# A third scratch tile for the swapped product, a fourth stage-matrix tile, and one reordered step in a long-convolution kernel

## The chip, the cores and the metric

The kernel runs on one core of a Trainium2 chip, in one launch. The metric is the device time of that launch in microseconds. Three runs of the kernel before took 1143.68, 1144.38 and 1144.84 us; the median, 1144.38 us, is the time before. The engines are called as in the profile: PE multiplies matrices (PEld is its weight loading), DVE, ACT and POOL work elementwise, and SP issues the DMAs.

## What is computed

For each of 8 batches, a causal convolution of 6400 positions by 128 channels with a filter of the same length, written in the reference with Fourier transforms, then a 5-tap convolution along the sequence whose sigmoid gates a projection, and an output projection:

```python
Yf = np.fft.rfft(x, n=2 * S, axis=1) * np.fft.rfft(h, n=2 * S, axis=0)[None]
y = np.fft.irfft(Yf, n=2 * S, axis=1)[:, :S, :]
for k in range(K):
    gate_pre += conv_w[k][None, None, :] * yp[:, k:k + S, :]
out = (1 / (1 + np.exp(-gate_pre)) * (y @ w_val)) @ w_out
```

Here `yp` is `y` with four rows of zeros ahead. Everything is float32.

## The kernel before, in words

The 6400 positions are laid out as 100 by 64, and the transform and its inverse are done as matrix products of size 100 and 64.

**Forward, first stage** (`Forward.group`, 16 groups for each batch): PE multiplies a group of input channels with the table `r1`; ACT and DVE copy the result into the big tile `gy`. **Forward, second stage and product** (`Product`, 13 blocks of 8 frequencies for each batch, the last one of 4): PE multiplies `gy` with the stage matrix of the block, a 512 KB tile that a DMA brings into one of the `m2_sb` tiles (`m2_load`). The result lies in a pair of PSUM banks (`ps2`, two pairs). Then it is multiplied with the filter's spectrum as complex numbers: `swap` (ACT, two instructions) writes the result with halves exchanged into a scratch tile `w_t`; `mul_u` (DVE) multiplies the PSUM pair with the first half of the spectrum into `gy`; `mul_t` (DVE) multiplies the scratch in place with the second half; `add` (POOL, on DVE for the last block) adds the scratch to `gy`. The two halves of the spectrum come by DMA from DRAM into two of the four `h_sb` tiles (`h_load`). `mul_u` waits for `swap`, since both read the same PSUM pair, and the block after the next needs that pair, so it waits for `mul_u`.

**Inverse, first stage** (`s3_quad`, 32 for each batch): PE multiplies `gy` with `r3`, and ACT and DVE copy the result into the tile `dt`. These are run in one loop with the forward groups of the next batch. **Inverse, last stage, and gates** (`Chunk`, 13 chunks of rows: the head (rows 60 to 63) first, then 12 chunks of 5 rows): `s4` is the last stage of the inverse, 8 or 10 pairs of PE instructions into one of four single PSUM banks (`ps1`). `copies` (ACT) writes the first tap into the gate's cells, the result `y` itself, and for all but the head a fourth tap into a tile `p_t`. `taps` (DVE, three instructions, more at borders) adds taps to the cells, and ends with an addition of `p_t` on POOL. `project` (PE) multiplies `y` with w_val, `sigm` (ACT) takes the sigmoid of the cells, `gate` (DVE) multiplies the two, `output` (PE) multiplies with w_out, and `store` copies the result out of PSUM with ACT and sends it out by DMA.

Where `y` and the gate's cells lie depends on `LATE`. Rows below it use places in `dt` that the chunk has already read; rows from it on use the tiles `yl_*` and `gl`, since the next batch's inverse begins to fill `dt` while their chunks are still at work.

The loop over chunks (steps `s` = 0 to 12) writes the order of every engine by hand; each engine runs its instructions in that order. In step `s` stand the product's PE part of block `s + 1` with a load of the stage matrix `M2B` blocks further on, `project` of chunk `s - 2`, `s4` of chunk `s`, `output` of chunk `s - 3`, `store` of `s - 4`, `swap` of block `s + 1`, `sigm` of `s - 2`, `copies` of `s`, `mul_u` of block `s`, `taps` of `s - 1`, `mul_t` and `add` of block `s`, the spectrum's load for block `s + 2`, and `gate` of `s - 2`. Step 0 has blocks 0 and 1. The products belong to the next batch, so the last of the eight batches has none. What is left of the last chunks (`finish`) is run between the first groups of the next batch.

The head of the program does the filter's own transform (`Spectrum`, 13 blocks) and the first batch's products in one loop of 13 steps, with four PSUM pairs; `hd` in DRAM keeps the spectrum.

Of the kernel before, what the change touches and what calls it, by code (L numbers as in the profile page):

```python
# [9 lines left out]
F32 = mybir.dt.float32  # L10
# [5 lines left out]
C = 128  # L16
N1 = 100
# [3 lines left out]
KB = 8  # L21
# [6 lines left out]
CH = 5  # L28
HEAD = (60, 4)
CHUNKS = [HEAD] + [(a, CH) for a in range(0, 60, CH)]  # L30
NCH = len(CHUNKS)
OUT_ORDER = CHUNKS[1:] + [HEAD]
LATE = 30
LATER = 7
M2B = 3
HB = 4
XB = 4

# [62 lines left out]
def longconv_moe(ctx: ExitStack, tc: tile.TileContext, x, h, r1, m2, r3, m4, w64, out):  # L101
# [4 lines left out]
    cp = ctx.enter_context(tc.tile_pool(name="cp", bufs=1))  # L106
# [12 lines left out]
    w_sb = cp.tile([C, NW], F32, name="w_sb")  # L119
    wc_sb = w_sb[:, 2 * C :]  # L120
    gl = cp.tile([128, N2 - LATE, N1], F32, name="gl")
    yl = {a: cp.tile([128, CH, N1], F32, name=f"yl_{a}") for a, _ in CHUNKS if a >= LATE}
    m2_sb = [cp.tile([128, KB, C], F32, name=f"m2_{i}") for i in range(M2B)]
    h_sb = [cp.tile([128, KB * C], F32, name=f"h_{i}") for i in range(HB)]
    x_sb = [cp.tile([PX, XG, N2], F32, name=f"x_{i}") for i in range(XB)]
    w_t = [cp.tile([128, KB * C], F32, name=f"w_{i}") for i in range(2)]
    p_t = [cp.tile([128, CH, N1], F32, name=f"p_{i}") for i in range(2)]
    hd = dp.tile([NKB, 2, 2 * N2, KB * C], F32, name="hd")

# [70 lines left out]
    class Forward:  # L200


        def __init__(self, src, dst):
            self.src, self.dst, self.n, self.i = src, dst, 0, 0
# [31 lines left out]
    def count(kb):  # L236
        return min(KB, N1 - kb * KB)

    def m2_load(kb):
        if kb < NKB:  # L240
            n = count(kb)
            nc.sync.dma_start(m2_sb[kb % M2B][:, :n], m2[:, kb * KB : kb * KB + n])

    def h_load(kb):
        if kb < NKB:
            n = count(kb) * C
            for r in range(2):
                nc.sync.dma_start(h_sb[(2 * kb + r) % HB][:, :n], hd[kb, r, :, :n])

    def h_double(kb):  # L250
        n = count(kb) * C
        for r in range(2):
            nc.sync.dma_start(hd[kb, r, N2:, :n], hd[kb, r, :N2, :n])

    def kdt(t, kb):
        n = count(kb)
        return t[:, : n * C].rearrange("p (d k t) -> p d k t", k=n, t=2)

    def s2_mm(src, kb):
        pt = pair()  # L260
        n = count(kb)
        for k in range(n):
            nc.tensor.matmul(
                pt[:, k // 4, (k % 4) * C : (k % 4 + 1) * C],
                lhsT=m2_sb[kb % M2B][:, k, :],
                rhs=src[:, :, kb * KB + k],
                start=True,
                stop=True,
            )
        if n <= 4:  # L270
            return pt[:, 0, : n * C].rearrange("p (k d t) -> p d k t", t=2, d=C // 2)
        return pt.rearrange("p b (k d t) -> p d (b k) t", t=2, d=C // 2)
# [24 lines left out]
    class Product:  # L297
        def __init__(self, kb, h=None):
            self.kb, self.v = kb, s2_mm(gy, kb)
            self.t = kdt(w_t[kb % 2], kb)  # L300
            self.u = gy[:, :, kb * KB : kb * KB + count(kb)]
            self.h = [kdt(i, kb) for i in h or [h_sb[(2 * kb + r) % HB] for r in range(2)]]

# [14 lines left out]
    def s3_quad(d0):  # L318
        pt = single()
        for q in range(4):  # L320
            d = d0 + q
            nc.tensor.matmul(
                pt[:N1, q * 2 * N2 : (q + 1) * 2 * N2],
                lhsT=gy[:, d // 2, :, d % 2],
                rhs=r3_sb,
                start=True,
                stop=True,
            )
        o = dv[:N1, :, :, d0 : d0 + 4].rearrange("p n c d -> p (n c) d")
        return lambda e: e(o, pt[:N1].rearrange("p (d m) -> p m d", d=4))  # L330
# [6 lines left out]
    def cells(x, n):  # L337

        out, i = [], 0
        while i < n:  # L340
            y = x + i
            end = 4 if y < 4 else LATE if y < LATE else N2
            k = min(n - i, end - y)
            s = (y - 4) % N2
            out.append((i, gl[:, y - LATE : y - LATE + k] if y >= LATE else dv[:, s : s + k, 1, :N1]))
            i += k
        return out

    class Chunk:


        def __init__(self, b, ch):
            self.b, self.ch = b, ch
            a, n = ch
            self.y = yl[a][:, :n] if a >= LATE else dv[:, a : a + n, 0, :N1]

# [91 lines left out]
    for f in (fh, fx):  # L448
# [8 lines left out]
        if f is fh:  # L457
            next(wgen)
    for kb in range(M2B):
        m2_load(kb)  # L460
    nc.sync.dma_start(r3_sb, r3)
    sp, pr = {0: Spectrum(0)}, {}
    for kb in range(-1, NKB + 1):
        if 0 <= kb < NKB:
            pr[kb] = Product(kb, sp[kb].h)
            m2_load(kb + M2B)
        if kb + 2 < NKB:
# [40 lines left out]
    def m4_load(a, k):  # L508
        k = N2 + 1 if k == N2 else k
        nc.sync.dma_start(m4_sb[:, a:k], m4.rearrange("k (n t) -> k n t", t=N1)[:, a:k])  # L510
# [5 lines left out]
    for b in range(B):  # L516
        nxt = b + 1 < B


        if trail:  # L520
            trail.pop(0)()
        if nxt:
            for kb in range(M2B):
                m2_load(kb)
            for kb in range(2):
                h_load(kb)
        for g in range(NG):
            e = [s3_quad(8 * g), s3_quad(8 * g + 4)]
            f = fx.group() if nxt else []
            e[0](act)  # L530
            e[1](dve)
            for i in f:
                i(act if g % 2 else dve)
            if trail:
                trail.pop(0)()
            if b == 0:
                m4_load(4 * g, 4 * g + 4)
                if LATER + g < NKB:
                    h_double(LATER + g)
                next(wgen, None)  # L540
                next(wgen, None)
        for _ in wgen:
            pass
        if b + 2 < B:
            fx = Forward(x[b + 2], gy)


        gs = Gates(b)
        ps = {}
        for s in range(NCH):  # L550
            if s == 0:
                gs.cs[0].s4()
                if nxt:
                    ps[0] = Product(0)
                    m2_load(M2B)
                    ps[0].swap()
            if nxt and s + 1 < NKB:
                ps[s + 1] = Product(s + 1)
                m2_load(s + 1 + M2B)
            gs.each("project", s - 2)  # L560
            if s:
                gs.cs[s].s4()
            gs.each("output", s - 3)
            gs.each("store", s - 4)
            if s + 1 in ps:
                ps[s + 1].swap()
            gs.each("sigm", s - 2)
            gs.cs[s].copies()
            if nxt:
                ps[s].mul_u()  # L570
            if s:
                gs.cs[s - 1].taps()
            if nxt:
                ps[s].mul_t()
                ps.pop(s).add()
                h_load(s + 2)
            gs.each("gate", s - 2)
            if s == 10 and b + 2 < B:
                fx.load(XB)
        trail = [lambda s=s, gs=gs: gs.finish(s) for s in range(NCH, NCH + 5)]  # L580
# [46 lines left out]
```

## Time and profile before

| | |
|---|---|
| median of three runs | 1144.38 us |
| the profiled execution | 1145.32 us, of which 1143.5 us are the profile's span |
| PE busy | 1063.3 us (93%) |
| DVE busy | 835.2 us (73%) |
| ACT busy | 725.4 us (63%) |
| POOL busy | 410.9 us (36%) |
| mean granted clock of PE | 0.988 |

All instructions of the kernel are issued through one helper, so they all carry line 88 (89 in the changed kernel), and groups are told apart by engine, operation and tiles: `pt<-gy,m` is a product's PE part, `pt<-m_sb,dt` is `s4`, `pt<-dt,w_sb` with 500 elements is `project` or `output`, `w<-pt` is `swap`, `gy<-pt,h` is `mul_u`, `w<-w,h` is `mul_t`, `gy<-gy,w` is `add`. In the timeline a row has its start, its length, the engine, the operation with its tiles and shapes, the number of instructions merged in the row (a PE product counts twice), and in brackets how long the engine stood idle before it and what released it. A PE row's length reaches into the next row by a little, since matmuls are pipelined; the time from one row's start to the next is what a piece costs.

### The profile page before, as it was taken

The page shows a single profiled execution, that of the slowest core. Times are in us where ns is not written, and L with a number is a line of the kernel's source. Part 1 is how long each engine was busy: PE and PEld are TensorE (multiplying, and loading weights), DVE is VectorE, ACT ScalarE, POOL GpSimd, SP SyncE. Part 2 cuts the span into 40 slices and gives each one's busy share as a digit, 9 for nine tenths or more (in the row PEclk, how much of TensorE's full clock was granted, in tenths as well). Part 3 has the DMA queues.
Part 4 walks back from the last instruction along what each step waited for, and adds up shares of the span by engine and source line. Part 5 has one row for each costly group of instructions (what it writes and reads, how often), then busy time and mean ns, then how long its engine had stood idle before and what let it go on. Part 6 is the DMA issues. An engine that isn't in the chain of part 4 may idle for free.

```text
span 1143.5 us, 19606 instructions
## 1 busy us (share of the span) xinstructions
PE 1063.3 (93%) x7480; PEld 946.2 (83%) x7480; DVE 835.2 (73%) x1176; ACT 725.4 (63%) x1188; POOL 410.9 (36%) x220
## 2 busy tenths in 40 slices
PE   8987899999999899999999999999999999999998
PEld 8977898769988699777987699886997789876975
DVE  5799776975589755896569855887568956698375
ACT  5787347764478546774568655775567744786365
POOL 0044004750067301770047500773018700475022
PEclk9999899989999999999999999999999999999999
DMA  5696947974199634986279741997349862793012
GB/s 148 193 326 196 333 129 257 286 210 150 44 310 279 238 90 137 297 240 213 57 243 297 221 150 55 307 265 237 89 142 296 235 214 56 251 290 111 26 28 89
DMA packets 105163, 221.15 MB, mean 193 GB/s; under 512 B 40170, under 2 KB 49358, under 8 KB 104910
## 3 DMA queue, kind: packets, MB, share of 16 engines
q1 hardware_dynamic: 105070, 219.89, 60.6%
q8 instruction: 60, 0.98, 0.4%
q14 instruction: 33, 0.27, 0.1%
HBM read 183.42 MB, written 39.32 MB: 195 GB/s over the span
## 4 chain that ended last, share of the span: by engine, by line
PE 54%; ACT 18%; POOL 12%; DVE 9%; issue 4%; DMA 3%; POOLq 0%; DVEq 0%; SPq 0%; ACTq 0%
PE pt L88 54%; POOL gy L88 7%; ACT w L88 7%; DVE dt L88 4%; POOL dt L88 3%; ACT dt L88 3%; DVE gl L88 3%; DMA m<-m 2%; ACT yl L88 2%; ACT p L88 2%; ACT gl L88 2%; DVE gy L88 1%; ACT gy L88 1%; DVE w L88 1%; POOL gl L88 1%
## 5 line engine op out<-in xcount | busy, mean ns | idle before, releaser
L88 PEld LDWEIGHTS pt<-m_sb,dt 100*128 100x128 f32 x2048 | 242.7, 193 | 71.9 <-ACT dt L88 29.6
L88 POOL TENSOR_TENSOR gy<-gy,w 128x1024 f32<-128x1024 f32 x96 | 228.0, 2375 | 148.7 <-DVE w L88 141.1
L88 PE MATMUL pt<-m_sb,dt 100*128 100x100 f32 x2048 | 247.9, 277 | 24.9 <-ACT dt L88 14.5
L88 PEld LDWEIGHTS pt<-r_sb,gy 128*100 128x100 f32 x2048 | 240.3, 172 | 30.9 <-issue 20.6
L88 PE MATMUL pt<-r_sb,gy 128*100 128x128 f32 x2048 | 248.0, 274 | 15.2 <-DVE gy L88 8.9
L88 ACT COPY dt<-pt 100x512 f32<-100x512 f32 (+3 forms) x264 | 153.8, 582 | 160.5 <-PE pt L88 159.2
L88 PEld LDWEIGHTS pt<-gy,m 128*128 128x128 f32 x1600 | 196.7, 190 | 33.1 <-DVE gy L88 12.2
L88 PE MATMUL pt<-r_sb,x 100*128 100x200 f32 x1152 | 217.1, 336 | 4.5 <-DMA x<-hl 4.2
L88 PE MATMUL pt<-gy,m 128*128 128x128 f32 x1600 | 204.7, 280 | 10.8 <-DVE gy L88 10.8
L88 DVE COPY dt<-pt 100x512 f32<-100x512 f32 (+2 forms) x168 | 116.7, 695 | 123.4 <-PE pt L88 120.9
L88 PEld LDWEIGHTS pt<-r_sb,x 100*128 100x128 f32 x1152 | 194.0, 193 | 4.7 <-issue 4.7
L88 ACT COPY gy<-pt 64x400 f32<-64x400 f32 x256 | 124.4, 486 | 100.7 <-PE pt L88 98.5
L88 DVE COPY gy<-pt 64x400 f32<-64x400 f32 x256 | 146.5, 572 | 42.8 <-PE pt L88 40.3
L88 ACT ACTIVATE w<-pt 64x1024 f32<-64x1024 f32 (+1 forms) x104 | 102.7, 988 | 103.7 <-POOL gy L88 84.1
L88 POOL MEMSET dt<- 128x4 f32 x8 | 0.8, 106 | 419.8 <-PE pt L88 419.8
L88 DVE TENSOR_TENSOR gy<-pt,h 128x1024 f32<-128x1024 f32 (+1 forms) x100 | 117.5, 1174 | 46.2 <-ACT w L88 45.9
L88 DVE SCALAR_TENSOR_TENSOR gl<-pt,w_sb,gl 128x500 f32<-128x500 f32 (+3 forms) x192 | 126.3, 661 | 15.8 <-POOL gl L88 4.9
L88 POOL TENSOR_TENSOR gl<-gl,p 128x500 f32<-128x500 f32 (+1 forms) x56 | 99.2, 1772 | 84.0 <-DVE gl L88 81.6
L88 DVE SCALAR_TENSOR_TENSOR dt<-pt,w_sb,dt 128x500 f32<-128x500 f32 (+3 forms) x192 | 115.1, 617 | 12.6 <-POOL dt L88 5.2
L88 DVE TENSOR_TENSOR w<-w,h 128x1024 f32<-128x1024 f32 (+1 forms) x100 | 122.3, 1223 | 0.0
L88 POOL TENSOR_TENSOR dt<-dt,p 128x500 f32<-128x500 f32 (+3 forms) x56 | 85.7, 1531 | 73.3 <-DVE dt L88 61.5
L88 ACT COPY w<-pt 64x1024 f32<-64x1024 f32 (+1 forms) x104 | 101.0, 971 | 2.4
(31 smaller groups left out, 741.6 us busy)
## 6 DMA issues: line engine op xcount, KB each, us to landing
h<-hd SPq DMA_DIRECT2D x168, 512.0 KB, 5.7
m<-m SPq DMA_DIRECT2D x96, 512.0 KB, 5.4
x<-xl SPq DMA_DIRECT2D x128, 224.0 KB, 2.8
out<-dt SPq DMA_DIRECT2D x48, 250.0 KB, 5.2
out<-yl SPq DMA_DIRECT2D x48, 250.0 KB, 3.0
hd<-h SPq DMA_DIRECT2D x10, 512.0 KB, 4.9
x<-hl SPq DMA_DIRECT2D x16, 224.0 KB, 2.6
h<-hd SPq DMA_DIRECT2D x14, 256.0 KB, 4.5
```

The source lines that it names most:

```text
L88: return self._tc.keep_in_program_order(call(*args, **kwargs))
```

## The change

Three things change. `M2B` is 4 and `w_t` has three tiles instead of two (`WB`), so `swap` of a block uses the scratch of the block three before. To make room, `LATE` is 35 instead of 30: `gl` has 29 rows instead of 34, the tile `yl_30` is gone, and the chunk at row 30 keeps `y` and its cells in `dt`; the head's `yl` tile has 4 rows instead of 5. And in step 1 `s4` of chunk 1 stands ahead of the product's PE part of block 2.

```diff
-LATE = 30
+LATE = 35
 LATER = 7
-M2B = 3
+M2B = 4
+WB = 3
...
-    yl = {a: cp.tile([128, CH, N1], F32, name=f"yl_{a}") for a, _ in CHUNKS if a >= LATE}
+    yl = {a: cp.tile([128, n, N1], F32, name=f"yl_{a}") for a, n in CHUNKS if a >= LATE}
...
-    w_t = [cp.tile([128, KB * C], F32, name=f"w_{i}") for i in range(2)]
+    w_t = [cp.tile([128, KB * C], F32, name=f"w_{i}") for i in range(WB)]
...
-            self.t = kdt(w_t[kb % 2], kb)
+            self.t = kdt(w_t[kb % WB], kb)
...
+            if s == 1:
+                gs.cs[s].s4()
             if nxt and s + 1 < NKB:
                 ps[s + 1] = Product(s + 1)
                 m2_load(s + 1 + M2B)
             gs.each("project", s - 2)
-            if s:
+            if s > 1:
                 gs.cs[s].s4()
```

On PE, at the start of the second batch's chunk loop (steps 0 to 2; `pt1` is a single PSUM bank, `pt2` a pair, `m4_sb` the table of `s4`), there stands before:

```order
L88 MATMUL pt1_2134<-m4_sb_68,dt_67 128x100 x8
L88 MATMUL pt2_2143<-gy_66,m2_0_80 128x128 x8
L88 MATMUL pt2_2155<-gy_66,m2_1_81 128x128 x8
L88 MATMUL pt2_2176<-gy_66,m2_2_82 128x128 x8
L88 MATMUL pt1_2186<-m4_sb_68,dt_67 128x100 x10
L88 MATMUL pt2_2213<-gy_66,m2_0_80 128x128 x8
```

On PE, at the same place of the changed kernel, there stands:

```order
L89 MATMUL pt1_2136<-m4_sb_68,dt_67 128x100 x8
L89 MATMUL pt2_2145<-gy_66,m2_0_79 128x128 x8
L89 MATMUL pt2_2157<-gy_66,m2_1_80 128x128 x8
L89 MATMUL pt1_2178<-m4_sb_68,dt_67 128x100 x10
L89 MATMUL pt2_2189<-gy_66,m2_2_81 128x128 x8
L89 MATMUL pt2_2215<-gy_66,m2_3_82 128x128 x8
```

The ten pairs of the second chunk's last stage have moved ahead of the third block, and the fourth block reads a fourth stage-matrix tile, not the first one again.

On ACT, in steps 1 and 2 of the same loop (`w` is the scratch, `p` the fourth tap), there stands before:

```order
L88 ACTIVATE w_0_91<-pt2_2176 64x1024
L88 COPY w_0_91<-pt2_2176 64x1024
L88 ACTIVATE dt_67<-pt1_2186,w_sb_71 128x5x100
L88 COPY dt_67<-pt1_2186 128x5x100
L88 ACTIVATE p_0_93<-pt1_2186,w_sb_71 128x500
L88 ACTIVATE w_1_92<-pt2_2213 64x1024
```

On ACT, at the same place of the changed kernel, there stands:

```order
L89 ACTIVATE w_2_93<-pt2_2189 64x1024
L89 COPY w_2_93<-pt2_2189 64x1024
L89 ACTIVATE dt_67<-pt1_2178,w_sb_71 128x5x100
L89 COPY dt_67<-pt1_2178 128x5x100
L89 ACTIVATE p_0_94<-pt1_2178,w_sb_71 128x500
L89 ACTIVATE w_0_91<-pt2_2215 64x1024
```

The order on ACT is the same; the third block's `swap` writes a scratch of its own, and the fourth block's writes the first block's.

On SP, at the end of each batch's chunk loop (`xl` is the batch after the next, `out` the result), there stands before:

```order
L88 DMA x_3_90<-xl 112x512
L88 DMA out<-yl_30_74 128x500
L88 DMA out<-yl_35_75 128x500
L88 DMA out<-yl_40_76 128x500
L88 DMA m2_0_80<-m2 128x1024
```

On SP, at the same place of the changed kernel, there stands:

```order
L89 DMA x_3_90<-xl 112x512
L89 DMA out<-dt_67 640x1x100
L89 DMA out<-yl_35_74 128x500
L89 DMA out<-yl_40_75 128x500
L89 DMA m2_0_79<-m2 128x1024
```

The chunk at row 30 leaves from `dt`, in pieces of 100 numbers, at the place in the queue that its own tile had.

## The prediction

> **What bounds the kernel now.** I read the page first, then busy time by stretch, then PE in order of time through one batch's chunk loop, then the chain of waits there. Of the page's busy times:
>
> ```profile
> PE 1063.3 (93%) x7480; PEld 946.2 (83%) x7480; DVE 835.2 (73%) x1176; ACT 725.4 (63%) x1188; POOL 410.9 (36%) x220
> ```
>
> PE leads over the whole span, so at most some 80 us (1143.5 less 1063.3) can be won by filling its idle time. Where is it? Four stretches: the head's product loop, the opening of the second batch's chunk loop (from its first `s4` to block 8's product), the middle of that loop, and the opening in the first batch.
>
> ```profile
> core 0: us, PE busy (x) PEld busy (x) DVE busy (x) ACT busy (x) POOL busy (x), PEclk, DMA share, GB/s
> 55.50:119.50 64.00, 45.90 (x365) 44.15 (x363) 62.91 (x53) 48.72 (x50) 28.49 (x12) 0.92 0.81 262
> 307.93:349.18 41.25, 37.32 (x281) 33.07 (x281) 31.30 (x43) 31.54 (x47) 23.87 (x13) 1.00 0.80 264
> 349.18:372.22 23.04, 23.04 (x161) 19.37 (x160) 21.06 (x27) 19.18 (x29) 18.38 (x10) 1.00 0.93 276
> 171.35:213.92 42.57, 37.65 (x281) 33.13 (x281) 31.30 (x43) 32.87 (x48) 23.84 (x13) 1.00 0.78 260
> ```
>
> In the head DVE is busy for 62.91 of 64.00 us: DVE is the bound there. In the middle of the chunk loop PE is busy without a gap, four steps in 23.04 us, 5.76 each, while DVE needs 5.27, ACT 4.80 and POOL 4.60 (each sum by four). Only in the opening does no engine fill the stretch. These are PE's rows of it, with four rows of the full pace behind, and the loop's end:
>
> ```profile
> 307.93 2.00 PE L88 MATMUL pt<-m_sb,dt 100*128 100x100 f32 x16
> 309.87 3.96 PE L88 MATMUL pt<-gy,m 128*128 128x128 f32 x32
> 315.38 2.12 PE L88 MATMUL pt<-gy,m 128*128 128x128 f32 x16 [1.54 <-DVE gy L88]
> 317.33 2.37 PE L88 MATMUL pt<-m_sb,dt 100*128 100x100 f32 x20
> 319.54 2.04 PE L88 MATMUL pt<-gy,m 128*128 128x128 f32 x16
> ...
> 336.72 1.08 PE L88 MATMUL pt<-dt,w_sb 128*128 128x500 f32 x2 [0.21 <-DVE dt L88]
> 339.29 2.48 PE L88 MATMUL pt<-m_sb,dt 100*128 100x100 f32 x20 [1.49 <-ACT dt L88]
> ...
> 346.00 2.48 PE L88 MATMUL pt<-m_sb,dt 100*128 100x100 f32 x20 [0.68 <-ACT dt L88]
> ...
> 349.18 2.02 PE L88 MATMUL pt<-gy,m 128*128 128x128 f32 x16
> 351.03 1.00 PE L88 MATMUL pt<-dt,w_sb 128*128 128x500 f32 x2
> 351.87 2.37 PE L88 MATMUL pt<-m_sb,dt 100*128 100x100 f32 x20
> 354.08 1.03 PE L88 MATMUL pt<-dt,w_sb 128*128 128x500 f32 x2
> 354.94 2.00 PE L88 MATMUL pt<-gy,m 128*128 128x128 f32 x16
> ...
> 377.12 1.00 PE L88 MATMUL pt<-yl,w_sb 128*128 128x500 f32 x2
> 379.17 2.48 PE L88 MATMUL pt<-m_sb,dt 100*128 100x100 f32 x20 [1.05 <-ACT yl L88]
> ```
>
> PE stands idle four times in the opening. The third block's product waits 1.54 us for `mul_u` of block 0. The others wait for DVE and ACT, which are late. Why are they late? The chain of waits says it, and the list of who waited for whom sums it:
>
> ```profile
> 325.47 1.97 POOL dt L88
> 327.43 2.35 POOL gy L88
> 329.81 1.03 ACT w L88
> ```
>
> ```profile
> ACT w L88 <- POOL gy L88: 84.1, 74, 2.8
> PE pt L88 <- DMA m<-m: 8.9, 7, 2.8
> ```
>
> `add` on POOL (2.35) releases `swap` on ACT, because `swap` of block k+2 writes the scratch that `add` of block k reads. Behind that `swap` on ACT stand `sigm` and `copies`, which `gate` and `taps` on DVE wait for. ACT spends 84.1 us so.
>
> **The change part by part.** *The third scratch.* `swap` of block k+3 now waits for `add` of block k, a whole step sooner. The 84.1 us go from ACT. What is late next on ACT: `sigm` of a chunk waits for POOL's last tap, the row at 325.47, which ends before the `add` that `swap` waited for. So `sigm` can start 2.35 us sooner, with the `swap` (two instructions of about 1 us) already behind it. After that nothing but PE sets the pace, since each other engine needs under 5.3 us in a step of 5.76.
>
> *The moved `s4`.* The two blocks from 309.87 cost two times 1.88, to 313.7. `s4` of chunk 1 (317.33 to 319.54, 2.21) fills 313.7 to 315.9; the third block could start at 315.38, so it comes about 0.6 later than before, and the pair of them ends at 317.9 instead of 319.54. Behind the third block stand its `swap` (ACT) and, on SP, its stage-matrix load and the spectrum loads behind it: all 0.6 us later. The spectrum loads issued between 312 and 349 us land so long after their issue:
>
> ```profile
> DMA to landing us min/median/max: 4.2/5.9/7.8
> ```
>
> The load behind the moved one was issued at about 318 and is wanted by `mul_u` of block 3 at about 325.6; 318.5 and 7.8 is 326.3 at the worst, 0.7 late on DVE. PE wants that `mul_u`'s end only at 327.2, so it costs PE up to 0.3. DVE's own rows give the next limit:
>
> ```profile
> 319.65 1.21 DVE L88 TENSOR_TENSOR w<-w,h 128x1024 f32<-128x1024 f32 x1
> 321.12 1.23 DVE L88 TENSOR_TENSOR gy<-pt,h 128x1024 f32<-128x1024 f32 x1 [0.25 <-ACT w L88]
> ```
>
> `mul_u` of block 2 starts when `mul_t` is done, 320.87, and ends at 322.1; PE comes to the fifth block at 322.0. A wait of 0.1.
>
> *The opening's sum.* At the full pace a product costs 1.85 (349.18 to 351.03), `project` 0.84, `s4` 2.21, `output` 0.86. From the first `s4` to block 8 stand 8 products (14.8), 6 `s4` (13.3), the head's `s4` of 1.94 (307.93 to 309.87), 4 `project` (3.4) and 3 `output` (2.6): 36.0. With the waits just named, 0.1 and 0.3, and another 0.4 for the restarts I take 36.8. The gain is 41.25 less 36.8, 4.45 us, in each of the batches 1 to 6. Its bounds are 3.9 (PE's busy time of 37.32 kept, which counts pipelined ends) and 5.2 (the bare 36.0). The first batch's opening takes 42.57, so 5.8. Sum: 6 × 4.45 + 5.8 = 32.5.
>
> *The clock.* Batch 4 (the first is batch 0) lost more at the place that is 339.29 in batch 1:
>
> ```profile
> 737.35 4.38 PE L88 MATMUL pt<-m_sb,dt 100*128 100x100 f32 x20 [1.49 <-ACT dt L88]
> ```
>
> ```profile
> 732.00:744.50 12.50, 10.80 (x51) 8.65 (x50) 11.18 (x15) 9.74 (x15) 9.29 (x5) 0.73 0.87 272
> ```
>
> The same ten pairs take 4.38 instead of 2.48, and the granted clock of that stretch is 0.73. I take it that PE's idle time just ahead lowered it. With the idle time gone the 1.9 us go too. The Trainium skill ("TensorE: Matmul & The Clock Gate", Part 1) says that the clock falls after an idle window of about 3.4 us; here it fell after gaps of 1.49 and 0.21 us, so by that rule the slow stretch isn't owed to them and the 1.9 us would stay: 1114.4 in place of 1112.5.
>
> *The loop's end.* In the changed build `project` of chunk 10 (377.12 here) waits for the `store` that `s4` of chunk 12 (379.17) waited for, so the idle time comes one piece earlier, 0.84 us, with ACT about 0.5 us sooner. I charge 0.35 us in each of 7 batches: −2.4. Bounds: −0.84 and +1.05 for each.
>
> *The fourth stage-matrix tile.* PE waited for these loads 8.9 us, all in the head. DVE hides it there (62.91 of 64.00). I cost it at nothing; without that cover it would be a gain of up to 8.9. In the chunk loop no wait for `m` stands in the list. At the start of each batch one more load of 512 KB goes ahead of the `x` loads on SP, which are issued four groups early.
>
> *`LATE` at 35.* The same instructions, other places. The chunk at row 30 leaves from `dt`, so the first copy of the next batch's inverse into `dt` now waits for that transfer:
>
> ```profile
> 374.06 9.83 SPq L88 DMA_DIRECT2D out<-yl  x3
> 386.44 0.58 ACT L88 COPY dt<-pt 100x512 f32<-100x512 f32 x1 [2.39 <-PE pt L88]
> ```
>
> ```profile
> out<-dt SPq DMA_DIRECT2D x48, 250.0 KB, 5.2
> ```
>
> Issued at 374.06 and 5.2 long it lands at 379.3, 7.1 us ahead. Nothing; without the cover 1 us in each of 7 batches for each microsecond late.
>
> *Sum.* 32.5 + 1.9 − 2.4 = 32.0. The profiled execution took 1145.3 us (1143.5 of span), so it would take 1113.3. It lies 0.9 above the median of the runs, so the forecast is **1112.5 us**. About 0.2%, 2.3 us, is what a measurement of this kernel can tell from no change.
>
> **The rivals.** *Transfers become the bound of the opening* (chance 0.2). The DMA share is 0.80 over 41.25 us, 33 us of work, nearly all of it behind block 0's product at 312; an opening of 36.8 leaves 32.7 us for it. For: the share is 0.93 even at the full pace. Against: a spectrum tile is asked for two steps before it is wanted, less the 1.2 us of `mul_u`: 7.1 us at the shortest steps (4.16, from 315.38 to 319.54), 10.3 at the full pace, and 7.8 is the longest landing. If landings grow by 2 us, some 1.7 us of each opening come back: 12 us, 1124.
>
> *The wait only moves to `sigm`* (0.05): POOL's tap is as late as its `add` was, and only the 1.54 us of the moved `s4` are won, 7 times, 10.8: 1133.5. Against: the tap's row ends 2.35 us before the `add`'s.
>
> *DVE and POOL collide* (0.03), the case that ends slower. One row each at the head's end:
>
> ```profile
> 115.84 2.37 POOL L88 TENSOR_TENSOR gy<-gy,w 128x1024 f32<-128x1024 f32 x1 [1.47 <-DVE w L88]
> 116.24 2.52 DVE L88 TENSOR_TENSOR w<-w,h 128x512 f32<-128x512 f32 x1
> ```
>
> A `mul_t` of half size, so at most 1.21, took 2.52 while POOL's `add` ran: 1.3 or more lost. If every `mul_t` met an `add` so, DVE's step would be 6.6 against PE's 5.76, 0.8 × 12 steps × 7 batches = 67 us, on top of 1112.5: 1179.5. It decides from 0.4 us a step (32.0 + 2.3, over 84 steps), where DVE's step passes 6.2. Against: `mul_t` of two blocks lie a DVE step of 5.3 apart and `add` follows the first at once with 2.37, so POOL must fall 2.5 us behind. The Trainium skill ("SBUF — State Buffer", Who interferes with whom) has it that a DVE instruction with two SBUF inputs and a POOL instruction that reads SBUF lock each other out for a whole instruction; the two rows agree.
>
> *The change does nothing* (0.02): the opening is bound by PE after all, 1144. The idle times in brackets speak against it.
>
> **How the numbers follow.** My forecast has the remaining 0.70; 1112.5 is its value. Its own bounds: openings at 5.2 (+4.5), the first batch's likewise 0.8, the loop's end at nothing (+2.4): 1105 with them; 3.9 instead of 4.45 and the clock not regained: 1118. To hold 8 in 10 I reach down to 1104 and up into the transfers' case, 1126. Faster by over 0.2%: 0.95 (0.70 + 0.2 + 0.05); within: 0.02; slower: 0.03.
>
> **What would show it.** Right: in the changed trace no wait of ACT `w` for POOL `gy` in the chunk loop; PE from the first `s4` to block 8 in about 36.8 us; the head unchanged at 64 us though the wait for `m` is gone; no slow clock in an opening. Wrong: DVE waits for `h` transfers in the openings, a `mul_t` much over 1.22, or the first ACT `dt` copy of a batch waiting for `out`.

## The result and the profile after

| | before | after |
|---|---|---|
| median, us | 1144.03 (1142.93 to 1144.84) | 1119.32 (1117.42 to 1120.04) |
| the profiled execution, its span | 1145.32, 1143.5 | 1117.42, 1115.5 |
| mean granted clock | 0.988 | 0.992 |

The ratio is 0.9776, with a 95% interval of 0.9763 to 0.979: 24.7 us less by the medians, 27.9 by the profiled executions; 1112.5 had been forecast, with a range from 1104 to 1126. The comparison of the profiles goes by the 27.9. The other three runs of the changed kernel took 1.4 to 2.6 us more than its profiled one; they have no trace, so where these lie stays open.

The page's busy times, and three stretches with the columns of the prediction's table: the head, the second batch's opening, and the first batch's opening.

```profile
PE 1053.5 (94%) x7480; PEld 942.9 (85%) x7480; DVE 831.8 (75%) x1176; ACT 729.7 (65%) x1188; POOL 410.7 (37%) x220
```

```profile
54.00:119.00 65.00, 45.82 (x372) 43.65 (x371) 62.90 (x53) 49.26 (x51) 28.47 (x12) 0.93 0.79 252
301.80:338.46 36.66, 36.60 (x281) 33.16 (x281) 30.16 (x42) 32.07 (x47) 23.14 (x13) 1.00 0.84 281
171.29:209.28 37.99, 36.73 (x280) 33.17 (x281) 31.45 (x44) 33.39 (x48) 24.42 (x13) 1.00 0.82 279
```

PE's share of the span is 94%, 93% before. The opening is 36.66 us long, and PE is busy for 36.60 of them. The head is still DVE's, 62.90 us of work. PE's rows of the opening, up to block 8's product, carry no idle time in brackets:

```profile
301.80 2.00 PE L89 MATMUL pt<-m_sb,dt 100*128 100x100 f32 x16
303.74 3.96 PE L89 MATMUL pt<-gy,m 128*128 128x128 f32 x32
307.54 2.37 PE L89 MATMUL pt<-m_sb,dt 100*128 100x100 f32 x20
309.75 3.90 PE L89 MATMUL pt<-gy,m 128*128 128x128 f32 x32
...
338.46 2.00 PE L89 MATMUL pt<-gy,m 128*128 128x128 f32 x16
```

The moved `s4` stands at 307.54, and the third block starts 7.95 us after the first row, where it started 7.45 after it. In the list of waits ACT's wait for POOL's `add` is gone, and ACT's `swap` waits for PE instead. PE's waits for ACT's `dt` copies fell from 19.6 to 9.4 us, but those for ACT's `yl` copies rose from 15.7 to 19.1:

```profile
ACT w L89 <- PE pt L89: 40.4, 57, 2.2
PE pt L89 <- ACT yl L89: 19.1, 20, 1.4
PE pt L89 <- ACT dt L89: 9.4, 15, 1.2
```

Nearly all of these waits of PE lie at the loop's end, from block 12 on:

```profile
361.50 1.08 PE L89 MATMUL pt<-gy,m 128*128 128x128 f32 x8
363.07 1.11 PE L89 MATMUL pt<-yl,w_sb 128*128 128x500 f32 x2 [0.49 <-ACT dt L89]
364.02 2.37 PE L89 MATMUL pt<-m_sb,dt 100*128 100x100 f32 x20
...
368.67 1.10 PE L89 MATMUL pt<-yl,w_sb 128*128 128x500 f32 x2 [1.41 <-ACT yl L89]
...
373.92 1.11 PE L89 MATMUL pt<-yl,w_sb 128*128 128x500 f32 x2 [1.08 <-ACT yl L89]
...
377.42 1.12 PE L89 MATMUL pt<-r_sb,gy 128*100 128x128 f32 x8 [0.68 <-ACT dt L89]
```

Three `project`s wait there (chunks 9, 10 and 11), where before `s4` of chunk 12 and the `project` of chunk 11 waited, 1.05 and 1.08 us; the quad's wait was there before, too. From block 12 to the next batch's first `s4` the changed kernel takes 69.47 us in every full batch, the kernel before 68.41: each end lost 1.06.

Added up by stretches of the two profiles: six openings 27.7 us (4.57 each, 4.84 in the last of them), the first opening 4.6, the slow clock in batch 4 1.8, seven loop ends −7.4, a slow clock in batch 0's end that is gone 2.6, a slow clock in the last batch that is new −1.3: 28.0, the difference of the spans.

### The profile page after: what moved, and what is told of

Same layout as the page of the kernel before. It is cut to its first block, busy times and chain, and to the rows that moved or that the text cites. A ratio compares the mean times of both kernels' runs of the same rounds, so it can differ in the third digit from the quotient of the medians.

```text
span 1115.5 us, 19581 instructions
## 1 busy us (share of the span) xinstructions
PE 1053.5 (94%) x7480; PEld 942.9 (85%) x7480; DVE 831.8 (75%) x1176; ACT 729.7 (65%) x1188; POOL 410.7 (37%) x220
## 4 chain that ended last, share of the span: by engine, by line
PE 82%; ACT 9%; DVE 5%; issue 2%; DMA 1%; POOL 0%; POOLq 0%; ACTq 0%; SPq 0%; DVEq 0%
PE pt L89 82%; ACT yl L89 2%; ACT w L89 2%; ACT dt L89 2%; DVE w L89 1%; ACT p L89 1%; DVE gy L89 1%; ACT gl L89 1%; ACT gy L89 1%; DVE h L89 1%; DVE dt L89 1%; DVE gl L89 0%; DMA x<-xl 0%; DMA x<-hl 0%; POOL dt L89 0%
## 5 line engine op out<-in xcount | busy, mean ns | idle before, releaser
L89 ACT COPY dt<-pt 100x512 f32<-100x512 f32 (+3 forms) x280 | 163.1, 583 | 164.4 <-PE pt L89 163.1
L89 PE MATMUL pt<-m_sb,dt 100*128 100x100 f32 x2048 | 243.7, 274 | 3.5 <-DVE dt L89 2.6
L89 PE MATMUL pt<-gy,m 128*128 128x128 f32 x1600 | 201.7, 279 | 2.1 <-DVE dt L89 1.6
L89 DVE SCALAR_TENSOR_TENSOR dt<-pt,w_sb,dt 128x500 f32<-128x500 f32 (+7 forms) x216 | 132.6, 630 | 11.4 <-POOL dt L89 5.3
L89 DVE SCALAR_TENSOR_TENSOR gl<-pt,w_sb,gl 128x500 f32<-128x500 f32 (+2 forms) x168 | 108.8, 651 | 22.1 <-issue 9.9
L89 POOL TENSOR_TENSOR dt<-dt,p 128x500 f32<-128x500 f32 (+1 forms) x64 | 101.4, 1585 | 52.5 <-DVE dt L89 40.5
L89 PE MATMUL pt<-dt,w_sb 128*128 128x500 f32 (+2 forms) x240 | 115.3, 571 | 1.2 <-ACT dt L89 1.2
L89 POOL TENSOR_TENSOR gl<-gl,p 128x500 f32<-128x500 f32 (+1 forms) x48 | 83.2, 1734 | 74.7 <-DVE gl L89 73.7
```

Of the source, the lines that this page charges most:

```text
L89: return self._tc.keep_in_program_order(call(*args, **kwargs))
```

## The experiments

Each is the changed kernel but for its edit (9, 10 and 12 have those of 5 and 6 too), and ratios are to the kernel before, which was run beside each (medians 1144.2 to 1144.7 us).

| kernel | median, us | ratio, 95% interval |
|---|---|---|
| 1: two scratch tiles | 1144.61 | 0.9999, 0.9986 to 1.0012 |
| 2: `s4` in its old place | 1126.29 | 0.9836, 0.9817 to 0.9856 |
| 3: three stage-matrix tiles | 1119.56 | 0.9782, 0.9767 to 0.9797 |
| 4: the same, `LATE` at 30 | 1118.66 | 0.9772, 0.9758 to 0.9786 |
| 5: `s4` ahead at the end | 1108.61 | 0.9700, 0.9684 to 0.9715 |
| 6: one table load | 1115.06 | 0.9752, 0.9737 to 0.9768 |
| 7: banks by role | 1140.05 | 0.9965, 0.9945 to 0.9985 |
| 8: 7 with 6 | 1139.94 | 0.9962, 0.9943 to 0.9981 |
| 9: table of banks, with 5 and 6 | 1133.35 | 0.9908, 0.9886 to 0.9931 |
| 10: 5 with 6 | 1108.89 | 0.9686, 0.9668 to 0.9704 |
| 11: table of banks alone | 1144.53 | 0.9993, 0.9977 to 1.0008 |
| 12: 9, its table mended | 1102.53 | 0.9637, 0.9623 to 0.9650 |

**1, two scratch tiles.**

```diff
-WB = 3
+WB = 2
```

> The changed kernel with two scratch tiles again; the moved `s4`, the fourth stage-matrix tile and `LATE` at 35 stay. Theory (the opening was a loop of `swap`, taps and `add` that the third scratch opens): ACT waits for POOL's `add` again (some 80 us), each opening is as long as before (about 41 us for batches 1 to 6), and the moved `s4` only fills time that the loop then gives back elsewhere: 1144, give or take 3. Rival (each wait of PE was worth its own length): the moved `s4` alone wins the 1.54 us ahead of the third block in each of 7 batches, 10.8 in all: 1133.

The theory holds. PE's rows of the second batch's opening:

```profile
317.69 2.37 PE L89 MATMUL pt<-m_sb,dt 100*128 100x100 f32 x20
320.47 2.11 PE L89 MATMUL pt<-gy,m 128*128 128x128 f32 x16 [0.41 <-DVE gy L89]
...
331.41 1.11 PE L89 MATMUL pt<-dt,w_sb 128*128 128x400 f32 x4 [0.45 <-DVE dt L89]
...
337.37 2.48 PE L89 MATMUL pt<-m_sb,dt 100*128 100x100 f32 x20 [1.50 <-ACT dt L89]
...
344.08 2.48 PE L89 MATMUL pt<-m_sb,dt 100*128 100x100 f32 x20 [0.68 <-ACT dt L89]
...
347.26 2.00 PE L89 MATMUL pt<-gy,m 128*128 128x128 f32 x16
```

The 1.54 us ahead of the third block are filled, and the opening (from 306.01 to block 8 at 347.26) takes 41.25 us, to the hundredth what it took before: the time comes back in the later waits. ACT waits 93.6 us for POOL's `add`. What bounds the opening with two scratch tiles is the loop through `swap`, taps and `add`, and PE's idle time is what the loop leaves over.

**2, `s4` of chunk 1 back in its old place.**

```diff
-            if s == 1:
-                gs.cs[s].s4()
...
-            if s > 1:
+            if s:
                 gs.cs[s].s4()
```

> The changed kernel with `s4` of the second chunk back behind the third block's product; three scratch tiles stay. Theory: the wait of about 1.5 us ahead of the third block (its buffer pair is freed by `mul_u` of block 0, which nothing but an earlier start could hasten) stays in every opening and PE cannot make it up, since it is the bound behind it: 1.5 x 7 = 10.5 us slower than the changed kernel, 1130. Rival (the scratch tile is the whole gain, since the rest of the opening has slack): 1119 to 1121.

The wait is there again, and now costs time, since PE is the bound behind it:

```profile
308.41 2.12 PE L89 MATMUL pt<-gy,m 128*128 128x128 f32 x16 [1.54 <-DVE gy L89]
```

A batch takes 130.50 us from first `s4` to first `s4`, the changed kernel 129.18: 1.32 for a wait of 1.54, since a few tenths of other waits go. That makes six times 1.32; the first batch's opening is only 0.16 longer. By the medians it is 7.0 us, less than the 10.5 expected. So the scratch alone wins 18.1 us, the moved `s4` nothing without it and 7 with it.

**3 and 4, the two sizes.**

```diff
-M2B = 4
+M2B = 3
```

> The changed kernel with three stage-matrix tiles. Theory: the loads come in time in the chunk loop with three as well, and in the head DVE hides PE's wait for them, which returns at about 9 us without moving the head's end: 1119.3, give or take 1.5. Rival (with the faster openings the load of a block comes late when only three tiles are there): PE waits for the stage matrices in the openings, up to 1 us in each of 6: up to 1126.

```diff
-LATE = 35
+LATE = 30
-M2B = 4
+M2B = 3
```

> The changed kernel with three stage-matrix tiles and `LATE` at 30, so that only the third scratch and the moved `s4` are left of the change. Theory: the 1.06 us that each loop's end lost come from which PSUM bank each product takes there and from the short 13th block, not from `LATE`: 1119.3, give or take 2. Rival (the chunk at row 30, written with a stride into `dt` since `LATE` is 35, costs the loop's end): the ends are as short as before, up to 1 us in each of 7 batches less, 1112 to 1114.

Both theories hold: 1119.56 and 1118.66 beside 1119.32. With three tiles PE waits for the matrices again, all in the head, and DVE hides it:

```profile
PE pt L89 <- DMA m<-m: 8.3, 6, 2.6
```

With `LATE` at 30 the ends still take 69.49 us, so `LATE` is not what they lost by. Experiments 1 and 2 tell more: with two scratch tiles an end takes 68.62 us, with three and `s4` in its old place 69.48. Most of the loss comes with the third scratch.

**5, `s4` ahead of `project` in the last two steps.**

```diff
+            late = nxt and s >= 11
+            if late:
+                gs.cs[s].s4()
             gs.each("project", s - 2)
-            if s > 1:
+            if s > 1 and not late:
                 gs.cs[s].s4()
```

> The changed kernel with `s4` ahead of `project` in steps 11 and 12 of the batches that have a next one; nothing else. Theory (the loop's end waits for a PSUM bank that ACT's `store` empties, and whichever of the two comes first is given that bank): the gaps of 0.49 and 1.41 us stand ahead of `s4` instead of `project`, nothing is won: 1119.3, give or take 1.5. Rival (PE only lacks work to fill the wait, as in the opening): both gaps are filled by `s4`, 1.9 us in each of 6 batches: 1108.

The theory is wrong: 1108.61. The first gap did move to `s4`, but the later ones shrank:

```profile
360.36 2.48 PE L89 MATMUL pt<-m_sb,dt 100*128 100x100 f32 x20 [0.50 <-ACT dt L89]
...
365.20 2.48 PE L89 MATMUL pt<-m_sb,dt 100*128 100x100 f32 x20 [0.67 <-ACT yl L89]
...
370.04 1.11 PE L89 MATMUL pt<-yl,w_sb 128*128 128x500 f32 x2 [0.67 <-ACT yl L89]
```

Why, the chain of waits of the changed kernel shows at this place (ACT's `gl`, `yl`, `p` are `copies`, its last piece `store`):

```profile
360.84 0.68 ACT gl L89
361.51 0.47 ACT yl L89
361.98 0.58 ACT p L89
362.56 0.47 ACT dt L89
363.03 0.04 issue
363.07 3.33 PE pt L89 x22
366.40 0.02 issue
366.43 0.68 ACT gl L89
```

It is a loop again: `project` waits for a bank that `store` empties, `s4` stands behind `project`, `copies` wait for `s4`, and the next `store` stands behind `copies`. The `copies` at 366.43 start 4.93 us behind block 12; with `s4` first they start 4.09 us behind it. The rival had the time right and its working not: the gaps were not filled whole. From block 12 to the next batch it takes 68.31 us instead of 69.47, some 8 us in seven batches; the rest of the 9.8 between the profiled spans lies in the head (1.6) and the last batch (0.2, with a slow clock in both traces).

**6, one table load.**

```diff
+    nc.gpsimd.memset(yl[60][:, :1, :1], 0.0)
+    nc.scalar.activation(yl[60][:, :1, :1], yl[60][:, :1, :1], AF.Sigmoid)
```

> The changed kernel with a sigmoid of one column at the start of the program, so that the table that ACT loads in the first batch's chunk loop (1.28 us) is loaded there already. Theory (that load makes the first opening 1.3 us longer than the others): the first batch goes from its first `s4` to block 12 in 59.7 us instead of 61.0; 1118. Rival (the first opening is longer for another reason, the stores of `h` or the loads of `m4`): it stays at 61.0, and the time at 1119.3.

ACT's and PE's rows of the changed kernel that this was about, in the first opening:

```profile
191.05 1.28 ACT L89 ACT_TABLE_LOAD   x1
```

```profile
199.50 1.11 PE L89 MATMUL pt<-dt,w_sb 128*128 128x500 f32 x2 [1.20 <-ACT dt L89]
```

Without that load the first opening is as short as the others:

```profile
172.01:208.75 36.74, 36.67 (x281) 33.18 (x281) 30.18 (x42) 32.15 (x47) 23.14 (x13) 1.00 0.83 280
```

The theory holds, 1.25 us. The medians differ by 4.3; what lies beyond the 1.25 no trace shows. The Trainium skill ("ScalarE: Activation LUTs", What ACT_TABLE_LOAD costs) has 1283 ns for the load itself, and the 1.28 agree; it adds some 1380 ns of drain, but here ACT's next instruction starts at 192.35, 0.02 us behind the load's end.

**7 and 8, banks by role.** The pool `ps1` gives each `s4`, `project` and `output` one of four PSUM banks. Here they are fixed (behind the loop `project` takes bank 1, `output` bank 2, the first quads 3 and 0):

```diff
-        return ps1.tile([128, 512], F32, name="pt1", tag="pt1")
+        return ps1[r].tile([128, 512], F32, name=f"pt1_{r}", tag=f"pt1_{r}")
...
+            pt = single(CHUNKS.index(self.ch) % 2)
...
+        def project(self, r=2):
...
+        def output(self, r=3):
```

> The changed kernel with its four single PSUM banks given out by role: `s4` takes two in turn, `project` and `output` one each, and behind the loop `project` takes a bank that the taps have emptied, and the two quads of a group take different ones. The same instructions in the same order. Theory (the gaps of the loop's end are waits for a bank, 0.49 + 1.41 + 1.08 us): the first two go, the third becomes a wait of about 0.3 us for `gate` of chunk 10, which must come first anyway; some 2.0 us in each of 6 or 7 batches: 1105 to 1107. Rival (DVE sets the loop's end: its `add` of block 12, 1.62 us, and the gates): the waits only change their names, 0.5 us in a batch at most: 1116 or more.

> Both together, the banks by role and the sigmoid at the start. Theory: the two gains add, since one lies in the first opening and the other behind block 12 of each batch: about 1.2 us below the kernel with the banks alone, 1104 to 1106. Rival (what the first opening wins, its end gives back): no faster than the banks alone.

Both theories fail, 1140, and the rival of 8 (no faster than 7) holds. At the end itself the banks did what was expected, 13.98 us from block 12 to the second quad instead of 15.92. But one bank for all `project`s is too few in the opening, where `gate` is late (38.42 us for an opening), and one for all `output`s too few behind the loop:

```profile
324.88 1.08 PE L89 MATMUL pt<-dt,w_sb 128*128 128x500 f32 x2 [1.67 <-DVE dt L89]
...
387.45 1.08 PE L89 MATMUL pt<-gl,w_sb 128*128 128x500 f32 x2 [2.08 <-ACT yl L89]
```

Behind the wait of 2.08 the clock falls in every second batch (below), and the last two batches together take 173.24 us instead of 167.82. In 8 the first batch takes 61.51 us to block 12, as in 7: the bank's wait stands where the table load's was.

**9, 10 and 11, a table of banks.** Up to chunk 7 the banks are those of the changed kernel; then (`project`, `output`) are:

```diff
+            k = CHUNKS.index(self.ch) or NCH
+            if k < 8 or self.b + 1 == B:
+                return 2 + k % 2, 2 + k % 2
+            return {8: (2, 3), 9: (2, 3), 10: (2, 2), 11: (1, 2), 12: (1, 3), 13: (1, 1)}[k]
...
+    QB = [(3, 0), (3, 0), (0, 2), (0, 3)] + [(1, 2), (0, 3)] * 6
```

> The changed kernel with `s4` ahead of `project` in steps 11 and 12, the sigmoid at the start, and banks by a table: up to chunk 7 each `project` and `output` take the banks they take in the changed kernel, from chunk 8 on `project` takes the bank that `gate` has emptied, in the last two chunks one that the taps have emptied, and no `output` behind the loop takes the bank of the `output` before it. Theory (each end is now held by waits for banks that ACT empties late, 0.50 + 0.67 + 0.67 us with the new order alone): these go, DVE (taps, the `add` of block 12, `gate` of chunk 10) is the next bound and leaves about 1 us of wait ahead of `output` of chunk 10; 1.2 us less in each of 6 ends than with the order and the sigmoid alone, some 1100. Rival (DVE sets the end already): no faster than those two.

> The changed kernel with `s4` ahead of `project` in steps 11 and 12 and the sigmoid at the start, banks as the compiler gives them. Theory (the traces: 1.17 us at each of 6 ends, 1.25 in the first opening): 1.3 us below the order alone, 1107. Rival (the medians: 10.7 and 4.3 us below the changed kernel, so more than those stretches show): the two add as they stand, 1104.

> The changed kernel with the table of banks alone, the order of the instructions as it was. Theory (the loss at the loop's end is one of banks): the waits of 0.49 and 1.41 us ahead of `project` go, about 1.0 ahead of `output` of chunk 10 and 0.8 ahead of the second quad stay; 1.7 us less in each of 6 ends, no loss in the openings: 1109. Rival (it was the order, and the banks don't matter): 1117 or more.

The theories of 9 and 11 fail: 1133.35 where some 1100 was expected, and 1144.53 where 1109 was. The end itself, from block 12 to the second quad, is 13.71 us in 9 and 13.99 in 11, and the openings are 36.66: that part holds. But the table gives the fifth group's first quad the bank of the head chunk's `output`, which ACT stores late. A row of 11 (its profiled execution, 1154.17, is the longest of twelve), and the stretches ahead of and behind that wait:

```profile
400.83 3.74 PE L89 MATMUL pt<-r_sb,gy 128*100 128x128 f32 x16 [2.57 <-ACT yl L89]
```

```profile
385.00:398.20 13.20, 12.93 (x81) 10.68 (x80) 7.51 (x13) 5.08 (x10) 0.00 (x0) 1.00 0.84 312
400.83:414.00 13.17, 13.17 (x80) 13.15 (x81) 4.94 (x9) 3.70 (x7) 0.00 (x0) 0.77 0.16 52
```

Besides, in the last batch, whose steps have no product, eight `project`s wait 1.38 to 1.56 us each for a `store`. One of them in 9, where it is the same:

```profile
1086.82 1.11 PE L89 MATMUL pt<-dt,w_sb 128*128 128x500 f32 x2 [1.41 <-ACT dt L89]
```

Number 10 came to 1108.89, neither theory's value: its first opening is 1.3 us shorter than that of 5 (36.71 and 38.02), but its head ended 1.4 us later and its last batch took 1.6 more. A gain of 1.3 us is below what these two stretches move from run to run.

**12, the table mended** (the edit is against 9; in the last batch the banks are those of the changed kernel).

```diff
-    QB = [(3, 0), (3, 0), (0, 2), (0, 3)] + [(1, 2), (0, 3)] * 6
+    QB = [(3, 0), (3, 0)] + [(0, 2), (0, 3)] * 2 + [(1, 2), (0, 3)] * 5
+    SL, PL, OL = "0120210210210", "-3102102102130", "-3333333332213"
...
+            if self.b + 1 == B:
+                return int(PL[k]), int(OL[k])
```

> The kernel with order, sigmoid and the table of banks, with the table mended at its two bad places: the fifth group's first quad takes the bank that the group before it emptied, not that of the last `output`, and in the last batch every product takes the bank that it takes in the changed kernel. Theory (the end's own waits were 13.71 us from block 12 to the second quad with the table, 14.76 with the order alone, and the 2.57 us wait of the fifth group, the slow clock behind it and the last batch's eight waits of 1.4 us were all that made the table lose): some 1.0 us in each of 6 ends below the order and the sigmoid alone, 1103. Rival (the waits that are left at the end, 1.23 and 0.78 us within 4 us, lower the clock by themselves): 1.5 to 2 us in each batch given back, 1109 or more.

The theory holds, 1102.53, 3.6% below the kernel before and the fastest here. PE's waits behind block 12, and the list's row for them, where ACT's copies had 19.1 us in the changed kernel:

```profile
370.35 1.08 PE L89 MATMUL pt<-gl,w_sb 128*128 128x500 f32 x2 [1.23 <-DVE gl L89]
...
373.08 1.09 PE L89 MATMUL pt<-r_sb,gy 128*100 128x128 f32 x8 [0.79 <-DVE gl L89]
```

```profile
PE pt L89 <- DVE gl L89: 16.2, 16, 1.6
```

DVE (`gate` of chunk 10, then the taps of chunk 12) now sets the end. A batch takes 127.13 us, against 128.01 in 10; batch 4 alone took 128.12, where one product waited 0.86 us for `mul_u`.

## Why the prediction was right, and what in it was not

*The number: inside the range partly by luck.* The prediction's own terms reached from 1105 to 1118 us, and the median is 1119.3. The stated range holds it only because it went up to 1126 for the case in which transfers bound the opening, which didn't occur. By the profiles the sum of 32.0 us became 28.0: the openings gave 1.0 more than forecast, the first opening 1.2 less, the loop's ends 5.0 less, and slow stretches that weren't forecast added 1.3. The rest is that the profiled execution lies 0.9 us above the median before and 1.9 below it after. (The prediction's last step, 1113.3 less 0.9, gives 1112.4 and not 1112.5.)

*The third scratch and the moved `s4`: right.* Forecast 36.8 us for an opening, 36.66 measured. Experiment 1 shows the mechanism: with two tiles the opening keeps its 41.25 us, though the moved `s4` fills PE's first wait. The prediction lumped scratch and move; apart they are 18.1 and 7.0 us of the medians.

*The first opening: a term mis-sized.* Forecast 5.8, measured 4.58. The step that failed took this batch's opening to end up as long as the others. The table load, 1.28 us on ACT, was hidden by the idle time and came to the front when that went; experiment 6 removed it, and the 1.25 us with it.

*The loop's end: the largest miss.* Forecast −2.4, bounded at −0.84 for each end; measured −7.4, 1.06 for each. The step had it that the idle time comes one piece earlier, with ACT about 0.5 us sooner. It took ACT's time as given, but behind the waiting `project` stands `s4`, behind that ACT's `copies`, and behind them the `store` that the next `project` waits for. Putting `s4` first (5) shortens the end by 1.16 us, and with other banks besides (12) by 2.03; `LATE` (4) does not.

*The clock: the size right, the cause borne out in part.* Batch 4 regained 1.8 us, forecast 1.9. The prediction laid the slow stretch to the idle time just ahead. The stretch at half clock begins at 737.62; in the 3.41 us ahead of it, which hold both waits, PE is busy for half the time:

```profile
734.21:737.62 3.41, 1.71 (x8) 0.73 (x7) 3.41 (x5) 3.07 (x6) 2.81 (x2) 1.00 0.71 247
737.62:741.03 3.41, 3.41 (x18) 3.41 (x18) 3.13 (x4) 1.76 (x2) 2.76 (x2) 0.50 0.85 220
```

The wait alone doesn't do it: batches 1 to 5 of the kernel before all have it, and so have those of experiment 1 (1.49 to 1.50 us each), and the clock fell behind one of the ten. The last section shows how it hangs on when a wait comes. Elsewhere the profiles gained 2.6 and lost 1.3 us by slow stretches that the forecast had left out. The row of the one lost, in the last batch:

```profile
1066.50:1076.00 9.50, 8.49 (x48) 6.86 (x49) 7.08 (x12) 4.36 (x8) 3.49 (x3) 0.82 0.11 27
```

*The costs at nothing: right.* The fourth stage-matrix tile (3) and `LATE` (4) change nothing that can be measured; in the head PE's wait for the matrices went, DVE's 62.90 us stayed, and the first `s4` starts at 171.29 us, 171.35 before.

*The rivals.* Transfers: the spectrum's loads land 6.3 us after their issue (median, 5.7 before), and in the chunk loops DVE waits for two of them, 0.5 and 0.1 us, which no opening shows. In 6 one such wait of 0.84 us made batch 3's opening 0.5 us longer, so the margin is thin. The wait moving to `sigm`: it would have left the openings long; its price was wrong besides, since experiment 1 shows that the moved `s4` alone wins nothing, not 10.8 us. DVE and POOL colliding: no `mul_t` of the chunk loops lies beside an `add`, but for one overlap of 0.1 us, since each `add` follows its own `mul_t` and ends before the next.

## What to carry to other kernels

Idle time of the bounding engine inside a loop of waits is not worth its length: fill it, and the loop gives it back further on. Look for the loop first (which instruction waits for a buffer that its own later work releases), open it with one more buffer or by putting the instruction that others wait for ahead of the one that waits; only then do the moves fill anything. When the opened stretch becomes tight, what it hid comes to the front at its end: look there for the next buffer that is released behind other work.

## What the runs showed of the hardware that was not expected

*Who comes first keeps the port.* A DVE and a POOL row of the changed kernel, and POOL's same tap where DVE does something else:

```profile
354.11 1.22 DVE L89 TENSOR_TENSOR w<-w,h 128x1024 f32<-128x1024 f32 x1
```

```profile
354.34 2.09 POOL L89 TENSOR_TENSOR gl<-gl,p 128x500 f32<-128x500 f32 x1 [1.04 <-DVE gl L89]
...
376.41 1.24 POOL L89 TENSOR_TENSOR gl<-gl,p 128x500 f32<-128x500 f32 x1 [4.19 <-DVE gl L89]
```

In 56 places of the chunk loops a tap of 128x500 meets a full `mul_t` that began about 0.25 us sooner; `mul_t` kept its 1.22 us each time, while the tap took 2.1 instead of 1.24. Where a tap of 128x200 began 0.08 us ahead of it (seven places), `mul_t` took 1.60. So it was in the prediction's row of the head: `add` began first, and `mul_t` took 2.52. The Trainium skill ("SBUF — State Buffer", Who interferes with whom) says that the order of issue decides which of the two is held; these rows agree.

*The clock falls after less than a whole idle window.* In experiment 7 the wait of 2.08 us stands in each of the middle batches, and the clock falls behind it in every second one, so the same wait costs 1.7 us more or nothing, by when it comes. The stretches at half clock show why. In all fourteen traces each of them, but for those that a trace's end cuts off, lasts 3.41 us or a multiple of it, and within a trace they begin on one grid of that step: in 7 at 388.85, 651.68 and 914.5 us, 77 steps apart each time. On this grid the wait of batch 1 lies nearly whole in one step, in which PE is busy for 1.40 us, and the clock of the next is half. That of batch 2 is split over two steps, busy for 2.67 and 2.09 us, and the clock stays:

```profile
385.44:388.85 3.41, 1.40 (x7) 0.95 (x8) 0.57 (x1) 2.27 (x5) 0.00 (x0) 1.00 1.04 370
388.85:392.27 3.42, 3.42 (x17) 3.42 (x16) 0.69 (x1) 1.06 (x2) 0.00 (x0) 0.50 0.27 98
...
518.56:521.97 3.41, 2.09 (x13) 1.64 (x14) 0.57 (x1) 1.69 (x5) 0.00 (x0) 1.00 1.02 340
521.97:525.38 3.41, 3.41 (x25) 3.10 (x24) 1.95 (x4) 0.96 (x2) 0.00 (x0) 1.00 0.28 68
```

Between the heads and the last 8 us of the traces, PE was idle for 32 to 75% of the step ahead of each fall. But four steps with 53 to 56% (in 8 and 9) had no fall behind them, so no threshold comes out. The Trainium skill ("TensorE: Matmul & The Clock Gate", Part 1) has a window of about 3.4 us that runs freely, and the grid agrees. It says that the clock falls after one idle window, and there these rows differ: no wait fills one.

*The head's length moves with the clock, but not with it alone.* The first batch's first `s4` starts between 169.1 and 175.4 us in the fourteen profiled executions, though the head differs in them by no more than a scratch tile, a stage-matrix tile and the one small sigmoid. The clock is at half in the head for 10.24 us in seven of them (169.1 to 171.9 us), for 13.65 in six (171.3 to 172.8) and for 17.06 in one (175.4). What moves it within these groups stays open.
